# Nine first-layer V batches in the load stage, and a ring of five tiles for the V rows

## The chip, the cores and the metric

The kernel runs on one core of a Trainium2 chip. Its time is the device time of one launch in microseconds (us), all loads of weights included. The engines are TensorE (PE; its weight loads are listed as PEld), VectorE (DVE), ScalarE (ACT), GpSimd (POOL) and the queue engine SyncE (SP). Each runs its own list of instructions in order. SP, ACT and POOL issue the DMA transfers.

## The reference

Two layers follow each other, with the same weights in both: a recurrent attention block A and a gated feed-forward block B, on 2048 rows of 512 columns in bf16.

```
def _A_ref(x, mem0, Wq, Wk, Wv, Wo, seg_len):       # H=32 heads, Dh=128, M=8, seg_len=32
    mem = mem0
    for s in range(n_seg):                          # 64 segments, one after the other
        h = concatenate([mem, xs], axis=1)          # 8 memory rows + 32 rows of x
        q, k, v = h @ Wq, h @ Wk, h @ Wv            # per head
        p = softmax(where(mask, q @ k^T * scale, -1e9))
        o = (p @ v) @ Wo
        mem = o[:, :M, :]                           # feeds the next segment
        outs.append(o[:, M:, :])
def _B_ref(x, ...):  return (sigmoid(x @ w_gate) * (x @ w_up)) @ w_down      # F = 1792

x = x + _A_ref(_layernorm(x), ...);  x = x + _B_ref(_layernorm(x), ...)      # layer 0
x = x + _A_ref(_layernorm(x), ...);  x = x + _B_ref(_layernorm(x), ...)      # layer 1
```

## The kernel before

**Steps.** Step t works on segment t of layer 0 and on segment t-6 of layer 1 together, so that one matmul streams 80 columns (40 of each layer). There are 70 steps. In steps 0 to 5 there is only layer 0, in steps 64 to 69 only layer 1. A step computes q and k (line 681, "QK"), the scores (700), the softmax on DVE and ACT (710 to 739), the transposed probabilities (750), the product with V (763, "PV") and the product with Wo (780), in five groups of six heads and one of two. It ends with the 8 memory rows, which step t+1 needs (line 793 or 798): the steps form a chain. Four segments are a block of 128 rows; a block's feed-forward (lines 844 and 863) and its layer norms run between the steps as filler.

**V.** Of a segment's 40 rows, 16 (the 8 memory rows and the first 8 of x) get their V in the step itself (the "strips", line 653). The other 24 rows per segment (96 per block) are computed ahead, for 128 rows at a time: a V pass (`v_pass`) is 8 evictions, and each eviction is 4 matmuls of 128x512 (line 557), a cast of 512 columns to a tile `vst`, and one or two DMAs (line 565) to a DRAM buffer `scr`. A step's rows come back by the loads `vsb<-scr` (line 643) into the tile `vsb`, from which PV takes its weights; the strips come from the tile `sst` (line 662). The buffers scr0 and scr1 belong to layers 0 and 1.

Layer 0's V rows can be computed at any time, since they need only the input x. Four blocks (384 rows) make three passes, a `v_group`. Before the change, groups [0,1,2,3] and [4,5,7,8] are written while the weights load ("boot"), and group [10,11,13,14] is given out after step 19. Blocks 6, 9, 12 and 15 fill the free 32 rows of layer 1's passes. In the boot stage the passes also use the six halves of the tiles `wd` as eviction buffers (`bootp`), and ACT issues the DMAs to scr instead of SP.

**Layer 1's V** is made just in time: block b's rows come out of layer 0's feed-forward, are normed, and the pass with tile `xvl` runs around the start of step 4b+6, which is also the step that first reads them. So in these steps V goes PE, cast, DMA to scr, DMA to vsb, PV.

**What sets the order.** Every piece of work is a task with an engine, a duration and a latency written in the code. A planner (`Planner`) places the tasks in ten rounds of list scheduling and keeps the round with the shortest planned span; the program is written in that order. For a DMA task the code gives the time until the data are there: 3500 ns for a write to scr (4500 in the boot stage), 3000 ns for a load of vsb. An engine's list is fixed: what is placed behind a waiting instruction waits too.

**DMA semaphores.** The DMAs of SP and ACT share eight semaphores (DMAHW0 to DMAHW7 in the rows below), given out in turn in the order of the program. A DMA is issued only when the one eight places ahead of it has landed.

Of the kernel before, what the change touches and what calls it, by code (L numbers as in the profile page):

```python
# [10 lines left out]
F32 = mybir.dt.float32  # L11
# [39 lines left out]
class Task:  # L51
    __slots__ = ("eng", "dur", "lat", "fn", "deps", "succ", "tail", "boost", "ndep", "ready", "start", "idx", "on", "fresh", "acq", "rel", "durs", "tick")

# [27 lines left out]
class Planner:  # L81
# [119 lines left out]
    def forward(self):  # L201
        T = self.tasks
        for bf in self.bufs:
            bf.first, bf.left, bf.slot, bf.t_free = None, len(set(bf.users)), None, 0.0
            bf.pool.free = [(0.0, None, i) for i in range(len(bf.pool.tiles))]
            bf.pool.used = {}
        free = {"PE": 0.0, "ACT": 0.0, "DVE": 0.0, "POOL": 0.0, "SP": 0.0}
        ready = {e: [] for e in free}
# [21 lines left out]
        for tk in T:  # L230
            tk.ndep = len(tk.deps)
            tk.ready = 0.0
            tk.on = None
            if tk.ndep == 0:
                release(tk)
# [5 lines left out]
        while left:  # L241
# [6 lines left out]
            for e in free:  # L248
# [19 lines left out]
                tk.tick = seq[e]  # L268
                if e in ("DVE", "ACT"):
                    end = now + tk.dur + self.WAIT * (self.waits(tk, seen[e]) > 1)  # L270
                else:
                    end = now + tk.dur
                free[e] = end
                heapq.heappush(events, (end, 1, 0))
                for bf in tk.acq:
                    pool = bf.pool
                    q = min((q for q in pool.free if self.slot_at(q, tk) <= now), key=lambda q: q[0])
                    pool.free.remove(q)
                    bf.slot = q[2]
                    bf.t_prev = q[1]  # L280
                    pool.used[bf.kind] = pool.used.get(bf.kind, 0) + 1
                for bf in tk.rel:
                    bf.left -= 1
# [30 lines left out]
    def waits(self, tk, seen):  # L314

        T = self.tasks
        need = {}
        for d in [T[i] for i in tk.deps]:
# [15 lines left out]
class Kern:  # L334
# [48 lines left out]
    def setup_tiles(self):  # L383
# [52 lines left out]
    def setup_consts(self):  # L436
        nc, tc = self.nc, self.tc
        with tc.tile_pool(name="tmp0", bufs=1) as tp0:
            identf = tp0.tile([P, P], F32, name="identf")
            cmasks.make_identity(nc, identf[:])  # L440
            nc.vector.tensor_copy(out=self.ident[:], in_=identf[:])
        NEG = -1.0e9 / self.scale
# [17 lines left out]
        for t_ in self.pb:  # L460
            nc.vector.memset(t_[:], 0.0)
        nc.gpsimd.memset(self.vsb[:], 0.0)

    def load_weights(self):
# [6 lines left out]
        def ld(dst, src, ns, keys):  # L471
            pl.add("SP", ns, lambda: nc.sync.dma_start(out=dst, in_=src), w=keys, boost=self.boot())

        for h0 in range(0, self.H, 8):
            cs = slice(h0 * P, (h0 + 8) * P)
            ld(self.wv[:, :, cs], wv_v[:, :, cs], P * self.DC * 8 * P * 2 / 300.0, [("wv", h) for h in range(h0, h0 + 8)])
        for g, (h0, gsz, us) in enumerate(self.groups):
            cs = slice(h0 * P, (h0 + gsz) * P)
            nb = P * self.DC * gsz * P * 2
            for nm, sb, v in (("wq", self.wq, wq_v), ("wk", self.wk, wk_v)):  # L480
                ld(sb[:, :, cs], v[:, :, cs], nb / 230.0, [(nm, h) for h in range(h0, h0 + gsz)])
            ld(self.wo[:, h0:h0 + gsz, :], wo_v[:, h0:h0 + gsz, :], P * gsz * self.D * 2 / 230.0, [("wo", h) for h in range(h0, h0 + gsz)])

# [22 lines left out]

    def layernorm_T(self, xb, xkey):
        nc, pl, D, DC = self.nc, self.pl, self.D, self.DC
        i = self.nxt("lns", 3)
        ln = self.lns[i]  # L510
        lk = ("lns", i)
        xn = pl.buf(self.xnp)
        pl.add("DVE", dve_ns(D), lambda: nc.vector.bn_stats(out=ln[:, 0:6], in_=xb), r=[xkey], w=[lk])
        pl.add("DVE", 100, lambda: nc.vector.bn_aggr(out=ln[:, 6:8], in_=ln[:, 0:6]), r=[lk], w=[lk])
# [4 lines left out]
        pl.add("ACT", act_ns(D) + 294, lambda: nc.scalar.activation(out=xn[:, :], in_=xb, func=ACTF.Identity, bias=ln[:, 10:11], scale=ln[:, 9:10]),  # L519
               r=[xkey, lk], w=[xn])  # L520
        B = pl.buf(self.bank, "bg")
# [26 lines left out]
    def v_pass(self, tile, keys, pieces, boot=False):  # L548

        nc, pl, DC = self.nc, self.pl, self.DC  # L550
        for k in range(self.H // 4):
# [10 lines left out]
            for c0, j, b, r0, n in pieces:  # L562
                d = self.scr[j][b * BLK * XS:(b + 1) * BLK * XS, cs].rearrange("(i r) e -> i r e", i=BLK)[:, r0:r0 + n, :]
                pl.add("ACT" if boot else "SP", 430, lambda vs=vs, d=d, c0=c0, n=n, q=nc.scalar if boot else nc.sync: (
                    q.dma_start(out=d, in_=vs[c0:c0 + BLK * n, :]), None)[1], lat=3500.0 + 1000.0 * boot,
                       r=[vs] + (["boot"] if boot else []), w=[("vd", j, b, q, k) for q in range(r0 // 8, (r0 + n) // 8)])

    def v_group(self, blocks, psts, boot=False):
# [5 lines left out]
        for b, cut in zip(blocks, cuts):  # L574
            pst, B = psts[b] if b in psts else self.ln_x(b, boot)
            for q, c0, r0, n in cut:
# [8 lines left out]

    def ln_x(self, b, boot=False):
        nc, pl = self.nc, self.pl
        i = self.nxt("xp", 2)
        xb, key = self.xp[i], (("xo", 0) if i == 0 else "xp1")
        pl.add("SP", 430, lambda: nc.sync.dma_start(out=xb[:], in_=self.x_in[b * P:(b + 1) * P, :]), w=[key], boost=(2e7 if boot else 0.0))  # L590
        return self.layernorm_T(xb[:], key)

# [17 lines left out]
    def emit_step(self, t):  # L610
# [26 lines left out]
        for j in jobs:  # L637
            s = t - j * LAG
            b, i = s // BLK, s % BLK
            row = KOFF if j == 0 else JOFF  # L640
            for k in range(2):
                cs = slice(k * 2048, (k + 1) * 2048)
                pl.add("SP", 430, lambda j=j, s=s, row=row, cs=cs: nc.sync.dma_start(
                    out=self.vsb[row:row + XS, cs], in_=self.scr[j][s * XS:(s + 1) * XS, cs]),
                    r=[("vd", j, b, q, kk) for q in range(3) for kk in range(4 * k, 4 * k + 4)], w=[("vx", j, k)], lat=3000.0)
        vb = [pl.buf(self.bank), pl.buf(self.bank)]
# [9 lines left out]
        def add_strips():  # L656
# [4 lines left out]
            for i in range(4):  # L661
                pl.add("SP", 430, lambda i=i: nc.sync.dma_start(
                    out=self.vsb[32:64, i * 1024:(i + 1) * 1024], in_=sb[32 * i:32 * i + 32, :, :]),
                       r=[(sb, 0), (sb, 1)], w=[("vs", i)], lat=3000.0, use=[sb])

        WB = pl.buf(self.bank)
        for g, (h0, gsz, us) in enumerate(self.groups):
# [92 lines left out]
            def pvm(h0=h0, gsz=gsz, ptsb=ptsb, OB=OB):  # L760
                for hl in range(gsz):
                    h = h0 + hl
                    nc.tensor.matmul(OB[:, hl * ncol:(hl + 1) * ncol], lhsT=self.vsb[:, h * P:(h + 1) * P],  # L763
                                     rhs=ptsb[:, hl, 0:ncol], start=True, stop=True)

            kk = range(h0 // 4, (h0 + gsz - 1) // 4 + 1)
            pl.add("PE", gsz * mm_ns(ncol), pvm, r=[("ptsb", pi)] + [("vs", k) for k in sorted({k // 2 for k in kk})] + [("vx", j, k) for k in sorted({k // 4 for k in kk}) for j in jobs], w=[OB])
            oi = self.nxt("otsb", 2)
# [38 lines left out]
    def ffn(self, j, b):  # L807
# [24 lines left out]
        for jp in range(FC // 2):  # L832
            gi = self.nxt("wg", self.NG)
            wg, wu = self.wg[gi], self.wu[gi]
            fs = slice(jp * 2 * P, (jp + 1) * 2 * P)
            pl.add("POOL", 1000, lambda wg=wg, fs=fs: nc.gpsimd.dma_start(out=wg[:], in_=self.wgv[:, :, fs]), w=[("wg", gi)], lat=3000.0)  # L836
            pl.add("POOL", 1000, lambda wu=wu, fs=fs: nc.gpsimd.dma_start(out=wu[:], in_=self.wuv[:, :, fs]), w=[("wu", gi)], lat=3000.0)  # L837
            GB = pl.buf(self.bank, "bg")
# [16 lines left out]
        for ip in range(FC // 2):  # L855
            di = self.nxt("wd", self.ND)
            wd = self.wd[di]
            pl.add("POOL", 1000, lambda wd=wd, ip=ip: nc.gpsimd.dma_start(out=wd[:], in_=self.wdv[:, 2 * ip:2 * ip + 2, :]), w=[("wd", di)] + (["boot"] if self.cnt["wd"] <= self.ND else []), lat=3000.0)  # L858

# [26 lines left out]
    def trace(self):  # L886
        self.fill = {}
        self.load_mem0()
        p0 = self.pre1(0)
        p1 = self.pre1(1)  # L890
        self.load_weights()
# [89 lines left out]
```

## Time and profile before

| | |
|---|---|
| median of three runs | 2004.15 us (2001.04 to 2006.01) |
| the profiled execution | 2000.2 us, of which the span of the program's instructions is 1998.4 |
| mean granted TensorE clock | 0.977 |
| PE busy | 1832.3 us (92%) |
| DVE, ACT, POOL busy | 67%, 57%, 27% |
| DMA moved | 273.78 MB, 137 GB/s |
| the last matmul of step 0 | ends at 119.7 us |
| steps 1 to 69 | some 17 to 53 us each |

The page and the views are to be read as follows. A group's row gives busy time, mean duration and the idle time of its engine just before it with what ended it. Rows of a timeline give start and length; "ACTq" and "SPq" are the issuing of DMAs by those engines, in which the engine itself is idle. A windows row gives for a stretch of time the busy time of each engine, then the granted clock, the mean share of the DMA engines that was busy, and the bytes per time.

### The profile page before, as it was taken

What the parts mean: (1) busy time and instruction counts of PE and PEld (TensorE: products, weight loads), DVE (VectorE), ACT (ScalarE), POOL (GpSimd) and SP (SyncE); (2) the same over time, 40 slices, a digit from 0 to 9 for tenths busy, and PEclk for the clock granted to TensorE, in tenths of its full rate; (3) what the DMA queues carried; (4) which work ended last, traced back from release to release, by engine and by line L of the source; (5) the groups of instructions that cost most, each with busy time, mean ns of one, the idle gap of its engine ahead of it and who ended that gap; (6) DMA issues with size and microseconds to landing.
All of it is one profiled execution on the core that took longest, in us unless ns stands there. A gap on an engine that the chain in (4) does not pass through costs nothing.

```text
span 1998.4 us, 93783 instructions
## 1 busy us (share of the span) xinstructions
PE 1832.3 (92%) x40904; PEld 1581.0 (79%) x41116; DVE 1335.8 (67%) x4353; ACT 1139.4 (57%) x2628; POOL 545.5 (27%) x765
## 2 busy tenths in 40 slices
PE   5679899999999999899999999999999999999987
PEld 2368787888878787787988888888889887988775
DVE  5466577676766675665777766677667677766764
ACT  2145565565655665565666656566665666665553
POOL 2001103233322223222322223242314232333322
PEclk8889999999999999999999999999999999999998
DMA  7823315455544455545545446464536454455534
GB/s 241 271 61 84 103 48 148 137 142 156 138 123 124 128 148 167 144 112 145 145 123 142 132 110 178 112 185 118 149 90 171 130 142 139 121 162 133 158 101 117
DMA packets 124319, 273.78 MB, mean 137 GB/s; under 512 B 23034, under 2 KB 63746, under 8 KB 123906
## 3 DMA queue, kind: packets, MB, share of 16 engines
q0 software_dynamic: 53760, 176.20, 31.5%
q1 hardware_dynamic: 63234, 85.26, 15.2%
q8 instruction: 322, 5.28, 1.2%
q10 hardware_dynamic: 6912, 6.29, 0.9%
q14 instruction: 91, 0.75, 0.1%
HBM read 222.04 MB, written 27.26 MB: 125 GB/s over the span
## 4 chain that ended last, share of the span: by engine, by line
PE 66%; DMA 14%; DVE 8%; issue 5%; ACT 3%; POOL 2%; SPq 1%; ACTq 0%; DVEq 0%; POOLq 0%
PE bank L681 24%; PE bank L780 13%; PE bank L844 7%; PE bank L653 5%; DMA scr<-vst 4%; PE bank L557 4%; PE bank L763 3%; PE bank L700 3%; PE bank L750 3%; PE bank L863 2%; DMA vsb<-scr 2%; DMA scr<-wd 2%; DVE st L710 1%; DMA wd<-in_B_w_down_dram 1%; DMA vsb<-sst 1%
## 5 line engine op out<-in xcount | busy, mean ns | idle before, releaser
L681 PE MATMUL bank<-hT,wq_sb 128*128 128x80 bf16 (+1 forms) x8960 | 625.0, 198 | 9.2 <-issue 2.8
L681 PE MATMUL bank<-hT,wk_sb 128*128 128x80 bf16 (+1 forms) x8960 | 624.9, 198 | 3.6 <-issue 2.0
L921 ACT CAST qku<-bank 128x480 bf16<-128x480 f32 (+3 forms) x770 | 392.9, 512 | 265.3 <-PE bank L681 229.9
L681 PEld LDWEIGHTS <-wq_sb 128*128 128x128 bf16 x8960 | 458.8, 99 | 31.5 <-issue 13.7
L681 PEld LDWEIGHTS <-wk_sb 128*128 128x128 bf16 x8960 | 452.0, 99 | 3.1 <-DMA wk_sb<-in_A_Wk_dram 1.7
L710 DVE TENSOR_TENSOR st<-bank,maskb 64x240 f32<-64x240 f32 (+5 forms) x768 | 283.4, 371 | 199.3 <-PE bank L700 190.2
L780 PE MATMUL bank<-otsb,wo_sb 128*128 128x80 bf16 (+1 forms) x8960 | 375.4, 200 | 5.9 <-ACT otsb L921 3.0
L780 PEld LDWEIGHTS <-wo_sb 128*128 128x128 bf16 x8960 | 346.0, 101 | 18.3 <-issue 8.4
L836 POOL DMA_DIRECT2D wg<-in_B_w_gate_dram x224 | 170.4, 761 | 561.2 <-PE bank L844 487.1
L921 ACT CAST otsb<-bank 128x480 bf16<-128x480 f32 (+3 forms) x420 | 198.6, 487 | 133.4 <-PE bank L763 98.7
L858 POOL DMA_DIRECT2D wd<-in_B_w_down_dram x224 | 159.4, 713 | 272.0 <-PE bank L750 95.6
L720 ACT ACTIVATE st<-st 104x240 f32<-104x240 f32 (+5 forms) x420 | 160.5, 384 | 100.5 <-DVE st L717 81.6
L736 DVE TENSOR_TENSOR pb<-st,rz 104x480 bf16<-104x480 f32 x348 | 206.8, 597 | 11.4 <-PE bank L750 7.1
L516 POOL TENSOR_TENSOR lns<-lns,negh 128x1 f32<-128x1 f32 x78 | 44.8, 576 | 608.3 <-DVE lns L515 498.6
L700 PE MATMUL bank<-qku 128*128 128x80 bf16 (+1 forms) x2240 | 170.2, 199 | 26.0 <-ACT qku L921 23.6
L722 DVE TENSOR_REDUCE sm<-st 104x6 f32<-104x240 f32 (+5 forms) x420 | 153.8, 368 | 59.9 <-ACT st L720 57.5
L921 ACT CAST ptsb<-bank 128x480 bf16<-128x480 f32 (+2 forms) x288 | 145.0, 508 | 63.1 <-PE bank L750 52.6
L763 PE MATMUL bank<-ptsb,vsb 128*128 128x80 bf16 (+1 forms) x2240 | 141.9, 201 | 41.9 <-DMA vsb<-scr 25.6
L844 PE MATMUL bank<-xnT,wg 128*128 128x128 bf16 x1792 | 176.7, 222 | 3.0 <-ACT xnT L921 1.1
L844 PE MATMUL bank<-xnT,wu 128*128 128x128 bf16 x1792 | 176.2, 222 | 1.6 <-DMA wu<-in_B_w_up_dram 1.6
L700 PEld LDWEIGHTS <-qku 128*128 128x128 bf16 x2240 | 117.5, 99 | 69.8 <-issue 22.1
L837 POOL DMA_DIRECT2D wu<-in_B_w_up_dram x224 | 167.9, 750 | 2.4 <-PE bank L844 1.1
(80 smaller groups left out, 2502.4 us busy)
## 6 DMA issues: line engine op xcount, KB each, us to landing
wg<-in_B_w_gate_dram POOLq DMA_DIRECT2D x224, 256.0 KB, 4.6
wu<-in_B_w_up_dram POOLq DMA_DIRECT2D x224, 256.0 KB, 5.0
wd<-in_B_w_down_dram POOLq DMA_DIRECT2D x224, 256.0 KB, 4.9
vsb<-scr SPq DMA_DIRECT2D x256, 96.0 KB
vsb<-sst SPq DMA_DIRECT2D x280, 64.0 KB
scr<-vst SPq DMA_DIRECT2D x144, 96.0 KB
wv_sb<-in_A_Wv_dram SPq DMA_DIRECT2D x4, 1024.0 KB
wq_sb<-in_A_Wq_dram SPq DMA_DIRECT2D x5, 768.0 KB
```

The lines of the kernel that those rows point to most:

```text
L681: nc.tensor.matmul(o_ap, lhsT=W[:, c, h * P:(h + 1) * P], rhs=mv(c), start=(c == 0), stop=(c == DC - 1))
L700: nc.tensor.matmul(s_all(SB)[:, uh - h0 + i, :], lhsT=qku[:, i, 0, :], rhs=fview(qku[:, i, 1, q0:q0 + 1], qc), start=True, stop=True)
L710: pl.add("DVE", dve_ns(n, True), lambda gsz=gsz, hs=hs, st=st, SB=SB, pj_=pj_, npj_=npj_, idx=idx: nc.vector.tensor_tensor(out=st[pj_, hs] ...
L720: pl.add("ACT", act_ns(n), lambda hs=hs, st=st: nc.scalar.activation(out=st[pr, hs], in_=st[pr, hs], func=ACTF.Exp, scale=self.scale), r=s ...
L736: nc.vector.tensor_tensor(out=o, in0=st[pr, hs].unsqueeze(1).to_broadcast([npart, 2, gsz, L]), in1=rz[pr, :, 0:gsz].unsqueeze(3).to_broadc ...
L763: nc.tensor.matmul(OB[:, hl * ncol:(hl + 1) * ncol], lhsT=self.vsb[:, h * P:(h + 1) * P], rhs=ptsb[:, hl, 0:ncol], start=True, stop=True)
L780: nc.tensor.matmul(WB[:, c * ncol:(c + 1) * ncol], lhsT=self.wo[:, h, c * P:(c + 1) * P], rhs=otsb[:, hl, 0:ncol], start=(h == 0 and c == ...
L836: pl.add("POOL", 1000, lambda wg=wg, fs=fs: nc.gpsimd.dma_start(out=wg[:], in_=self.wgv[:, :, fs]), w=[("wg", gi)], lat=3000.0)
L837: pl.add("POOL", 1000, lambda wu=wu, fs=fs: nc.gpsimd.dma_start(out=wu[:], in_=self.wuv[:, :, fs]), w=[("wu", gi)], lat=3000.0)
L844: nc.tensor.matmul(gu[:, 2 * i + k, :], lhsT=W[:, c, i * P:(i + 1) * P], rhs=xnT[:, c, :], start=(c == 0), stop=(c == DC - 1))
L858: pl.add("POOL", 1000, lambda wd=wd, ip=ip: nc.gpsimd.dma_start(out=wd[:], in_=self.wdv[:, 2 * ip:2 * ip + 2, :]), w=[("wd", di)] + (["boo ...
L921: nc.scalar.copy(out=dst, in_=src)
```

## The change

Five things change together.

1. Group [10,11,13,14] is given out in the boot stage too, so that all nine passes stand there. Their x blocks are fetched ahead, between the loads of Wv, into tiles that are idle at that time (`xs2` to `xs5`, `xa`, `oxT1`, `hff`), where before two tiles took turns.
2. `vsb`, one tile of 4096 columns, becomes a ring of five tiles of 1024 columns (8 heads). Chunk k of step t lies in tile (4t+k) mod 5. The loads `vsb<-scr` are four of 48 KB per layer and step instead of two of 96 KB, and each PV group waits for its own chunks.
3. The first loads of the feed-forward's weights (`wg`, `wu`) wait for the last load of Wo.
4. The planner's numbers: a write to scr 2600 ns (4600 in boot), a load of vsb 6000, of sst 2600, Wq, Wk and Wo at 180 GB/s instead of 230, a POOL DMA 760 ns to issue and 4000 to land instead of 1000 and 3000.
5. The planner counts a wait for a buffer's earlier users (`prev`) among the waits of an instruction.

The core of the diff:

```diff
-        self.vsb = c.tile([P, HE], BF16, name="vsb")
+        self.vsb = [c.tile([P, 1024], BF16, name=f"vsb{i}") for i in range(5)]
...
+        xb = list(self.boot_x)
         for h0 in range(0, self.H, 8):
             cs = slice(h0 * P, (h0 + 8) * P)
             ld(self.wv[:, :, cs], wv_v[:, :, cs], P * self.DC * 8 * P * 2 / 300.0, [("wv", h) for h in range(h0, h0 + 8)])
+            for b in xb[:3]:
+                self.load_x(b, *self.boot_x[b])
+            xb = xb[3:]
...
-                ld(sb[:, :, cs], v[:, :, cs], nb / 230.0, [(nm, h) for h in range(h0, h0 + gsz)])
+                ld(sb[:, :, cs], v[:, :, cs], nb / 180.0, [(nm, h) for h in range(h0, h0 + gsz)])
...
-                    q.dma_start(out=d, in_=vs[c0:c0 + BLK * n, :]), None)[1], lat=3500.0 + 1000.0 * boot,
+                    q.dma_start(out=d, in_=vs[c0:c0 + BLK * n, :]), None)[1], lat=2600.0 + 2000.0 * boot,
...
-            for k in range(2):
-                cs = slice(k * 2048, (k + 1) * 2048)
-                pl.add("SP", 430, lambda j=j, s=s, row=row, cs=cs: nc.sync.dma_start(
-                    out=self.vsb[row:row + XS, cs], in_=self.scr[j][s * XS:(s + 1) * XS, cs]),
-                    r=[("vd", j, b, q, kk) for q in range(3) for kk in range(4 * k, 4 * k + 4)], w=[("vx", j, k)], lat=3000.0)
+            for k in range(4):
+                cs = slice(k * 1024, (k + 1) * 1024)
+                vu = (4 * t + k) % 5
+                pl.add("SP", 430, lambda j=j, s=s, row=row, cs=cs, vu=vu: nc.sync.dma_start(
+                    out=self.vsb[vu][row:row + XS, :], in_=self.scr[j][s * XS:(s + 1) * XS, cs]),
+                    r=[("vd", j, b, q, kk) for q in range(3) for kk in (2 * k, 2 * k + 1)], w=[("vx", j, vu)], lat=6000.0)
...
+            kk = [(4 * t + k) % 5 for k in range(h0 // 8, (h0 + gsz - 1) // 8 + 1)]
+            pl.add("PE", gsz * mm_ns(ncol), pvm, r=[("ptsb", pi)] + [("vs", k) for k in kk] + [("vx", j, k) for k in kk for j in jobs], w=[OB])
...
+            pl.add("POOL", 760, lambda wg=wg, fs=fs: nc.gpsimd.dma_start(out=wg[:], in_=self.wgv[:, :, fs]), r=[("wo", self.H - 1)], w=[("wg", gi)], lat=4000.0)
...
         self.v_group([4, 5, 7, 8], {}, True)
+        self.v_group([10, 11, 13, 14], {}, True)
...
-                if b == 4:
-                    self.v_group([10, 11, 13, 14], {})
```

What the planner makes of it is seen in three places of the programs. The first is ACT's list at the end of step 0: the last writes to scr (line 565 before, 572 after), the casts of q and k (`qku`, six heads are two casts of 6x40, the last two heads one cast of 4x40) and the exponential (`st`). Before:

```order
L565 DMA scr0_60<-wd0_133 96x512
L565 DMA scr0_60<-vst1_124 4x8x512
L565 DMA scr0_60<-vst1_124 96x512
L921 CAST qku2_80<-bank7_149 128x6x40
L921 CAST qku0_78<-bank4_146 128x6x40
L720 ACTIVATE st0_82<-st0_82 64x240
L921 CAST qku1_79<-bank5_147 128x4x40
L720 ACTIVATE st1_83<-st1_83 64x80
```

And after, at the same place:

```order
L940 CAST qku0_78<-bank5_151 128x6x40
L572 DMA scr0_60<-wd1_138 96x512
L572 DMA scr0_60<-wd2_139 4x8x512
L572 DMA scr0_60<-wd2_139 96x512
L572 DMA scr0_60<-wd0_137 4x8x512
L572 DMA scr0_60<-wd0_137 96x512
L572 DMA scr0_60<-vst0_127 4x8x512
L572 DMA scr0_60<-vst0_127 96x512
L735 ACTIVATE st0_86<-st0_86 64x240
L572 DMA scr0_60<-wd1_138 4x8x512
L572 DMA scr0_60<-wd1_138 96x512
```

The casts of the last group of six heads now stand ahead of the last eleven writes; behind the last write only the cast of the last two heads remains. Counted through the lists up to the last of these writes, ACT has 96 writes to scr before and 144 after. In the common order of all engines 75 of the 96 stand ahead of the last load of Wo, and 55 of the 144; so 21 stand behind it before, and 89 after, with 21 other ACT instructions among them (four before).

The second place is SP's list at step 26, where the group that is moved had its writes to scr0 (pieces of 4x16 rows, or of 96 and 4x8), next to those of layer 1's pass to scr1. Before:

```order
L565 DMA scr0_60<-vst1_124 4x16x512 [waits DMAHW6_49,DVE_49]
L565 DMA scr0_60<-vst1_124 4x16x512 [waits DMAHW7_49]
L565 DMA scr0_60<-vst2_125 4x8x512 [waits DMAHW0_49,Activation_49]
L565 DMA scr0_60<-vst2_125 96x512 [waits DMAHW1_49]
L565 DMA scr1_61<-vst0_123 96x512 [waits DMAHW2_49,DVE_49]
L565 DMA scr0_60<-vst0_123 4x8x512 [waits DMAHW3_49]
L662 DMA vsb_81<-sst0_126 32x1024 [waits DMAHW4_49,DVE_49,Activation_49]
```

And after, in the same step:

```order
L657 DMA vsb3_84<-scr0_60 24x1024 [waits DMAHW6_49,PE_49]
L572 DMA scr1_61<-vst1_128 96x512 [waits DMAHW7_49,Activation_49]
L572 DMA scr0_60<-vst1_128 4x8x512 [waits DMAHW0_49]
L572 DMA scr1_61<-vst2_129 96x512 [waits DMAHW1_49,Activation_49]
L657 DMA vsb4_85<-scr1_61 24x1024 [waits DMAHW7_49,DMAHW2_49,DMAHW1_49]
```

The group's writes are gone from there, and so are its 24 evictions and 96 matmuls on PE, which stood in steps 22 to 28; all nine passes now stand in step 0.

The third place is SP's list at step 30, one of the steps 4b+6 in which layer 1's V rows are made and read. Each eviction writes 96 rows to scr1 and 4x8 filler rows to scr0. Before:

```order
L565 DMA scr1_61<-vst0_123 96x512 [waits DMAHW5_49,Activation_49]
L643 DMA vsb_81<-scr1_61 24x2048 [waits DMAHW5_49,DMAHW6_49,DMAHW3_49,DMAHW1_49]
L565 DMA scr0_60<-vst0_123 4x8x512 [waits DMAHW7_49]
L565 DMA scr1_61<-vst1_124 96x512 [waits DMAHW0_49,Activation_49]
L565 DMA scr0_60<-vst1_124 4x8x512
L565 DMA scr1_61<-vst2_125 96x512 [waits DMAHW2_49,Activation_49]
L565 DMA scr0_60<-vst2_125 4x8x512
L565 DMA scr1_61<-vst0_123 96x512 [waits DMAHW4_49,DVE_49]
L565 DMA scr0_60<-vst0_123 4x8x512
L565 DMA scr1_61<-vst1_124 96x512 [waits DMAHW6_49,Activation_49]
L643 DMA vsb_81<-scr1_61 24x2048 [waits DMAHW6_49,DMAHW4_49,DMAHW7_49,DMAHW2_49,DMAHW0_49]
```

And after:

```order
L657 DMA vsb0_81<-scr1_61 24x1024 [waits DMAHW5_49,DMAHW4_49,DMAHW2_49]
L657 DMA vsb4_85<-scr1_61 24x1024 [waits DMAHW6_49]
L572 DMA scr0_60<-vst1_128 4x8x512 [waits DMAHW7_49]
L572 DMA scr1_61<-vst2_129 96x512 [waits DMAHW0_49,Activation_49]
L572 DMA scr0_60<-vst2_129 4x8x512 [waits DMAHW1_49]
L572 DMA scr1_61<-vst0_127 96x512 [waits Activation_49]
L657 DMA vsb1_82<-scr1_61 24x1024 [waits DMAHW3_49,DMAHW2_49,DMAHW0_49]
L572 DMA scr0_60<-vst0_127 4x8x512
L572 DMA scr1_61<-vst1_128 96x512 [waits DMAHW5_49,Activation_49]
L572 DMA scr0_60<-vst1_128 4x8x512 [waits DMAHW6_49]
L572 DMA scr1_61<-vst2_129 96x512 [waits DMAHW7_49,Activation_49]
L657 DMA vsb2_83<-scr1_61 24x1024 [waits DMAHW7_49,DMAHW5_49]
```

Before, the first half is loaded after the fourth eviction and the second half after the eighth. After, the four chunks are loaded after the second, fourth, sixth and eighth (the last load stands nine rows further on), and the four strips' loads for this step, which stood between the first and the second eviction, now stand between the sixth and the eighth. On PE the pass itself starts earlier: its first eviction stands at the end of step 29 and its second at the start of step 30 (before: four matmuls at the start of step 30, and the other seven evictions through the first half of the step, the last one just ahead of the first PV).

More of the change, by code (lines that the diff above doesn't have):

```diff
@@ L233, in forward @@
             tk.on = None
+            tk.prev = []
             if tk.ndep == 0:
@@ L279, in forward @@
                     bf.slot = q[2]
-                    bf.t_prev = q[1]
+                    tk.prev += pool.last.get(q[2], [])
+                    pool.last[q[2]] = sorted(set(bf.users))
                     pool.used[bf.kind] = pool.used.get(bf.kind, 0) + 1
+                end = now + tk.dur
+                if self.waits(tk, seen[e]) > 1 and e in ("DVE", "ACT"):
+                    end += self.WAIT
+                free[e] = end
+                heapq.heappush(events, (end, 1, 0))
                 for bf in tk.rel:
@@ L461, in setup_consts @@
             nc.vector.memset(t_[:], 0.0)
-        nc.gpsimd.memset(self.vsb[:], 0.0)
+        for t_ in self.vsb:
+            nc.gpsimd.memset(t_[:], 0.0)
     def load_weights(self):
```

65 lines of the change are left out of this document (34 added, 31 removed).

## Prediction

> **What bounds the kernel now.** I read the page's head first, then busy time by stretches cut at step ends, then who waited for whom, then the timelines of ACT, SP and PE at the places of the change.
>
> ```profile
> span 1998.4 us, 93783 instructions
> PE 1832.3 (92%) x40904; PEld 1581.0 (79%) x41116; DVE 1335.8 (67%) x4353; ACT 1139.4 (57%) x2628; POOL 545.5 (27%) x765
> ```
>
> ```profile
> 0.00:119.70 119.70, 69.94 (x735) 38.70 (x745) 58.80 (x154) 23.92 (x52) 18.33 (x33) 0.84 0.71 232
> ...
> 543.00:906.80 363.80, 339.11 (x7146) 290.09 (x7184) 240.63 (x784) 212.82 (x472) 102.17 (x143) 0.99 0.49 136
> 906.80:1235.60 328.80, 315.36 (x7036) 279.73 (x7072) 231.70 (x752) 200.84 (x454) 100.32 (x139) 0.99 0.51 140
> 1235.60:1563.40 327.80, 312.47 (x7027) 276.61 (x7070) 229.47 (x753) 201.04 (x447) 99.84 (x138) 1.00 0.50 140
> ```
>
> After its label and length a row gives the busy time of PE, PEld, DVE, ACT and POOL, the clock, the DMA share and GB/s. The first row is step 0: PE is idle for 49.8 of 119.7 us and the DMA engines are 71% busy. The others are twelve steps each (18 to 29, 30 to 41, 42 to 53). There PE is busy 93 to 96% of the time, so work taken from PE's list there shortens the kernel. Steps 18 to 29 hold the group that is moved.
>
> ```profile
> PE bank L763 <- DMA vsb<-scr: 25.6, 16, 4.1
> PE bank L700 <- ACT qku L921: 23.6, 17, 6.6
> ```
>
> Past step 0 the largest wait of PE is the first row: PV stands for V rows on their way back from DRAM, 16 times, 1.6 us each, at most 4.1. The second row is mostly step 0, where ACT's casts stand behind ACT's own writes to scr.
>
> **The change part by part.**
>
> *The group leaves steps 22 to 28.* Steps 18 to 29 take 363.8 us, the next twelve, with the same recurrent and feed-forward work, 328.8: 35.0 us more. That splits into 23.75 us of PE busy time (339.11 less 315.36) and 11.25 of idle time (24.7 less 13.4). The V line alone shows the busy part:
>
> ```profile
> 543.00:906.80 363.80, 46.48 (x177) 17.14 (x192) 0.99 0.49 136
> 906.80:1235.60 328.80, 21.91 (x84) 8.14 (x96) 0.99 0.51 140
> ```
>
> 192 weight loads against 96: the 96 matmuls of the group take 24.6 us. The 24 casts, four layer norms and four x loads go too. I take all 35.0. Bounds: 23.75, if the extra idle time belongs to the planner's choice there, and 35.0.
>
> *The group comes into step 0.* PE has 49.8 us free for 24.6 us of matmuls, so PE is not what counts; ACT's list is. ACT issues every write to scr in this stage, and its casts and exponentials stand in the same list:
>
> ```profile
> 97.16 0.36 ACT L921 CAST qku<-bank 128x240 bf16<-128x240 f32 x1 [6.33 <-DMA scr<-wd]
> 97.23 0.60 ACTq L565 DMA_DIRECT2D scr<-wd  x1
> 97.88 0.36 ACT L921 CAST qku<-bank 128x240 bf16<-128x240 f32 x1 [0.37 <-issue]
> 97.94 0.40 ACTq L565 DMA_DIRECT2D scr<-wd  x1
> 98.43 1.19 ACTq L565 DMA_DIRECT2D scr<-vst  x2
> 99.71 1.11 ACTq L565 DMA_DIRECT2D scr<-wd  x2
> 101.05 1.11 ACTq L565 DMA_DIRECT2D scr<-vst  x2
> 102.42 0.60 ACTq L565 DMA_DIRECT2D scr<-wd  x1
> 103.07 0.40 ACT L720 ACTIVATE st<-st 64x240 f32<-64x240 f32 x1 [4.83 <-DMA scr<-wd]
> 103.36 0.31 ACTq L565 DMA_DIRECT2D scr<-wd  x1
> 103.77 1.09 ACTq L565 DMA_DIRECT2D scr<-vst  x2
> ```
>
> Here no weight is in flight any more, and ACT issues almost without a pause: 12 writes and three operations (1.12 us) in 7.70 us, 0.55 us for each write. So the issuing itself is the pace (median 0.526 us):
>
> ```profile
> L565 ACTq DMA_DIRECT2D scr<-wd x60: 310/526/691, 23.7 to 103.4; - x60
> ...
> L565 ACTq DMA_DIRECT2D scr<-vst x36: 310/526/1190, 18.2 to 104.4; - x36
> ```
>
> When do the weights end? The loads of Wq, Wk and Wo go out between these two rows of SP, at 275 GB/s:
>
> ```profile
> 24.17 0.38 SPq L472 DMA_DIRECT2D wq_sb<-in_A_Wq_dram  x1
> ...
> 87.93 0.37 SPq L472 DMA_DIRECT2D wo_sb<-in_A_Wo_dram  x1
> ```
>
> ```profile
> 24.10:88.30 64.20, 45.58 (x377) 22.91 (x382) 32.34 (x77) 11.98 (x24) 2.16 (x4) 0.87 0.83 275
> 88.30:104.90 16.60, 7.18 (x74) 3.50 (x75) 5.99 (x13) 1.48 (x4) 0.00 (x0) 0.79 0.56 174
> ```
>
> In the new order 55 writes instead of 68 lie between them (13 x 64 KB is 0.85 MB, 3 us less), and ahead of them six loads of gate and up weights go (1.57 MB) and four x blocks come (0.52 MB), 4 us less. So the last Wo load goes out near 81 us. Then 89 writes follow in ACT's list instead of 21: 89 x 0.55 is 49 us, the 21 ACT operations among them take 9 us (seven casts of 0.36, four exponentials of 0.40, three norms of 0.81 and others), and 2 us I add for waits while weights still land: the last write near 141 us instead of 104.9. After it the old order needed 14.8 us to the end of step 0, since the last group of six heads came behind it; the new order has only the last two heads behind it, as from this row on:
>
> ```profile
> 111.93 0.29 ACT L921 CAST qku<-bank 128x160 bf16<-128x160 f32 x1 [2.34 <-PE bank L681]
> ```
>
> From there to 119.7 it was 7.8 us; the transposes that stand ahead of the first PV now add some 2. Step 0 would end at 151 instead of 119.7: plus 31. Bounds: ACT without any wait from its first write at 18.2 us needs 144 x 0.55 and some 18 us of operations (of the 23.92 that it is busy in step 0), so ends at 115 us, and 10 more, plus 6; at the pace of the whole old tail (16.6 us for 21 writes, 0.79 us each) 81 + 70 + 10, plus 41.
>
> The Trainium skill (DMA: Bandwidth & Descriptors, Rules for kernel authors) says that DMAs of SP, ACT and GpSimd run on the same 16 engines, so that spreading them saves only issue time. By that rule the bytes would set the price of step 0, which is the first rival below; the 0.83 DMA share while weights load agrees with it, the 0.56 after them does not.
>
> *x fetched ahead.* Ten x loads move ahead of the weights on SP; counted above. It removes waits such as PE's for `xn`, which lie in step 0 and are covered by ACT's list: 0.
>
> *The ring.* In step 30, PV of heads 16 and up waited for the second half of vsb, which SP could issue only when the eighth eviction had landed in scr (SP's, then PE's timeline, then the chain):
>
> ```profile
> 933.54 0.29 SPq L643 DMA_DIRECT2D vsb<-scr  x1
> ```
>
> ```profile
> 933.83 0.31 PE L763 MATMUL bank<-ptsb,vsb 128*128 128x80 bf16 x4
> 937.79 1.09 PE L763 MATMUL bank<-ptsb,vsb 128*128 128x80 bf16 x14 [3.65 <-DMA vsb<-scr]
> ```
>
> ```profile
> 929.94 3.46 DMA scr<-vst
> 933.54 4.12 DMA vsb<-scr
> ```
>
> Now heads 16 to 23 need only six evictions, the pass starts in step 29, and the planner allows 8.6 us for the two transfers, which take 7.6 here (it allowed 6.5). I take two thirds of the 25.6 us as gone, minus 17. Not all, since the write and the load still follow each other with 7.6 us. Bounds: minus 25.6 and plus 25.6 (rival three).
>
> The skill's same section says to join small transfers, and that below 64 KB one pays mostly overhead: the ring's 48 KB loads go against it. By the rule a load would still take about the 4.12 us of the 96 KB one, so I count nothing for the smaller size.
>
> *SP, POOL, numbers.* SP gets up to four more issues per step of 0.29 us (the row above), 1.2 us where twelve steps take 328: hidden, unless SP stands (rival three). Gate and up loads start after Wo; step 4 is the first to use them, and the rest of step 0 with steps 1 to 3 is the cover. The planner's other numbers only move filler: within plus or minus 4.
>
> Sum: -35 + 31 - 17 = -21 us. On the profiled execution's 2000.2 us that is 1979; its own time lies 4 us under the median of the runs, 2004.15, so the median should come to 1983.
>
> **The rivals.**
>
> *Step 0 is limited by bytes, not by ACT.* 48 more writes of 64 KB and four x blocks less six weight loads are 2.1 MB, 8 us at 275 GB/s: -35 + 8 - 17 gives 1960. For it: the share of 0.83 while weights load. Against it: 89 of the 144 writes stand behind the last load, where the share was 0.56.
>
> *The stalls stay.* Evictions and the round trip through DRAM remain, and a stall that moves from the second half to a chunk is still a stall: -35 + 31 + 0 gives 2000, within what can be measured. For it: the 7.6 us of the two transfers in the chain, which the ring does not shorten. Against it: the pass starts earlier on PE, and the last wait shown was for the eighth eviction.
>
> *SP becomes the wait: slower.* In steps 4b+6 SP has four loads instead of two that stand until a write has landed, and all later writes, and the strips, stand behind them; with three tiles `vst` the casts then stand, and DVE and ACT with them. If the stalls double, +25.6: -35 + 31 + 26 gives 2026. It decides from 4 us of added stalls on. For it: 3.46 us per write, where the planner now counts 2.6. Against it: SP is otherwise far from full.
>
> **How the numbers follow.** The sum above has 0.48, with 1972 to 1996 as its own range; bytes 0.18; stalls stay 0.18; SP stands 0.16. What differs by less than 0.3%, about 6 us, can't be told from no change. So faster takes the first two cases and a sixth of the third, less 0.01: 0.68; same most of the third and a little of the fourth: 0.15; slower the rest, 0.17. The range goes from 1958 to 2006: it takes in the bytes case and the case in which the stalls stay, and leaves out the fourth and the outer bounds.
>
> **What would show it.** Right: step 0 ending near 150 us with ACT issuing scr writes at 0.55 us each up to about 140; twelve steps 18 to 29 of about 328 us; PE's wait for `vsb<-scr` below 12 us; the V line with 288 `xvf` matmuls all in step 0. Wrong: step 0 ending below 132 us (bytes), or PE waits for vsb, or casts waiting for `scr<-vst`, above 30 us in all (SP).

## The result and the profile after

The changed kernel takes 1946.7 us (median; 1945.5 to 1950.0) where the kernel before took 2003.2 beside it: a ratio of 0.972, interval 0.970 to 0.974. The forecast was 1983 with a range from 1958 to 2006. Faster was right; the gain is 56 us and not 21.

The head of the page after the change:

```profile
span 1948.3 us, 94182 instructions
PE 1817.5 (93%) x40901; PEld 1568.3 (80%) x41116; DVE 1327.0 (68%) x4329; ACT 1152.9 (59%) x2652; POOL 549.5 (28%) x769
```

Busy time by stretches, cut as before: step 0, steps 18 to 29, 30 to 41, 42 to 53.

```profile
0.00:148.25 148.25, 95.55 (x845) 48.65 (x857) 79.37 (x194) 28.13 (x62) 21.64 (x41) 0.85 0.67 213
559.70:885.20 325.50, 314.10 (x7035) 278.94 (x7074) 225.49 (x746) 207.15 (x461) 100.85 (x139) 0.99 0.51 142
885.20:1204.80 319.60, 311.51 (x7035) 276.28 (x7070) 228.78 (x749) 204.77 (x456) 100.81 (x139) 1.00 0.51 143
1204.80:1525.40 320.60, 312.32 (x7035) 276.73 (x7074) 223.92 (x741) 206.59 (x462) 100.68 (x138) 1.00 0.52 144
```

Step 0 is longer by 28.5 us and steps 18 to 29 are shorter by 38.3; both were forecast (31 and 35). But the stretches that the group never touched are shorter too, 319.6 for 328.8 and 320.6 for 327.8. In the list of PE's waits there is no row for `vsb<-scr` any more (25.6 us before). Of the rows that are left, the first lies in step 0 for the most part, and the largest for vsb is that of the strips:

```profile
PE bank L715 <- ACT qku L940: 20.1, 11, 8.8
...
PE bank L778 <- DMA vsb<-sst: 8.3, 13, 1.3
```

Something else went with the waits. These are four stretches of 3.4 us around the wait of 3.65 us in step 30 of the kernel before (busy time of PE, then the granted clock):

```profile
930.60:934.05 3.45, 3.40 (x62) 1.00 0.82 221
934.05:937.46 3.41, 0.09 (x3) 1.00 0.94 269
937.46:940.87 3.41, 3.08 (x42) 0.50 0.92 234
940.87:944.28 3.41, 3.36 (x81) 1.00 0.37 101
```

PE stands in the second. In the third it works, but at half the clock: 42 matmuls where the next stretch has 81. So this wait cost its own 3.65 us and then some 1.7 us more, half of a stretch. Before, steps 1 to 61 hold ten such half-clock stretches; after, two (one of double length).

With this the time of any stretch splits into three parts: PE's idle times of over 0.2 us, the clock lost (half of each half-clock stretch), and the rest, which I call work. The table is worked out in this way from the profiled execution of each kernel, in us; only the median is over all of its runs, and a single execution lies up to 8 us from it (e5: 1951 and 1959):

| kernel | median | step 0 | steps 1 to 61 | = work | + idle | + clock | steps 62 on |
|---|---|---|---|---|---|---|---|
| before | 2003 | 119.7 | 1661.7 | 1570.8 | 73.9 | 17.1 | 217.0 |
| after | 1947 | 148.3 | 1589.6 | 1542.6 | 41.9 | 5.1 | 210.4 |
| e2: after, old numbers | 2029 | 126.6 | 1693.6 | 1543.1 | 111.2 | 39.3 | 210.9 |
| e4: after, group late | 1960 | 123.5 | 1626.0 | 1561.8 | 52.2 | 11.9 | 209.0 |
| e5: before, vsb load 6000 | 1959 | 121.4 | 1617.6 | 1574.2 | 38.3 | 5.1 | 210.3 |
| e6: before, ring | 2016 | 122.1 | 1676.6 | 1568.6 | 84.1 | 23.9 | 217.1 |
| e8: after, 230 GB/s, no prev | 1934 | 130.3 | 1585.9 | 1548.9 | 31.9 | 5.1 | 211.5 |

The work of steps 30 to 61 alone lies between 836 and 845 us in all 17 kernels profiled, while these steps take 846 to 907. So the kernels differ by idle time and clock there, not by what PE has to do. From before to after steps 1 to 61 lose 28 us of work (the moved group), 32 of idle time and 12 of clock.

### The profile page after: what moved, and what is told of

It reads as the page before. It is cut to its first block, busy times and chain, and to the rows that moved or that the text cites. A ratio compares the mean times of both kernels' runs of the same rounds, so it can differ in the third digit from the quotient of the medians.

```text
span 1948.3 us, 94182 instructions
## 1 busy us (share of the span) xinstructions
PE 1817.5 (93%) x40901; PEld 1568.3 (80%) x41116; DVE 1327.0 (68%) x4329; ACT 1152.9 (59%) x2652; POOL 549.5 (28%) x769
## 4 chain that ended last, share of the span: by engine, by line
PE 75%; DVE 9%; DMA 7%; ACT 4%; issue 3%; POOL 1%; ACTq 1%; SPq 0%; DVEq 0%; POOLq 0%
PE bank L696 27%; PE bank L795 14%; PE bank L859 9%; PE bank L564 6%; PE bank L667 5%; PE bank L715 3%; PE bank L765 3%; PE bank L878 3%; PE bank L778 3%; DMA vsb<-sst 2%; DVE st L725 2%; DMA scr<-vst 1%; DVE mx L730 1%; DVE pb L751 1%; DVE sm L737 1%
## 5 line engine op out<-in xcount | busy, mean ns | idle before, releaser
L795 PEld LDWEIGHTS <-wo_sb 128*128 128x128 bf16 x8960 | 341.5, 99 | 20.6 <-issue 10.6
L940 ACT CAST ptsb<-bank 128x480 bf16<-128x480 f32 (+3 forms) x316 | 157.0, 503 | 55.5 <-PE bank L765 42.9
L715 PE MATMUL bank<-qku 128*128 128x80 bf16 (+1 forms) x2240 | 170.1, 199 | 20.8 <-ACT qku L940 20.1
L765 PE MATMUL bank<-ident,pb 128*128 128x80 bf16 (+1 forms) x2240 | 144.1, 198 | 20.3 <-DVE pb L754 15.8
```

Source lines behind the costliest of these rows:

```text
L715: nc.tensor.matmul(s_all(SB)[:, uh - h0 + i, :], lhsT=qku[:, i, 0, :], rhs=fview(qku[:, i, 1, q0:q0 + 1], qc), start=True, stop=True)
L765: nc.tensor.matmul(o_ap, lhsT=pb[:, hl, :], rhs=idn, start=True, stop=True)
L795: nc.tensor.matmul(WB[:, c * ncol:(c + 1) * ncol], lhsT=self.wo[:, h, c * P:(c + 1) * P], rhs=otsb[:, hl, 0:ncol], start=(h == 0 and c == ...
L940: nc.scalar.copy(out=dst, in_=src)
```

## The experiments

All of them compute the whole reference. Each was timed beside the kernel before, which had medians of 1999.8 to 2003.2 us.

### Which part brought the gain: four parts undone one at a time

My theory was the ring with the price of the clock added; the main rival was the planner's number for a load of vsb.

e1, the changed kernel with the single tile and its two loads of 96 KB, the number for a load still at 6000:

```diff
-        self.vsb = [c.tile([P, 1024], BF16, name=f"vsb{i}") for i in range(5)]
+        self.vsb = c.tile([P, HE], BF16, name="vsb")
...
-            for k in range(4):
-                cs = slice(k * 1024, (k + 1) * 1024)
+            for k in range(2):
+                cs = slice(k * 2048, (k + 1) * 2048)
```

> The changed kernel with the old single tile vsb (two loads of 96 KB per layer and step, PV of heads 16 and up behind the second half), all else as after the change, the planner's 6000 ns for a vsb load too. My theory (the ring took the stalls away, and each stall cost more than its wait, because the granted clock was halved for 3.4 us after it): PE's wait for vsb<-scr returns to 20 us or more, with six or more half-clock stretches between steps 6 and 62, and the time goes from 1947 to 1980 (1970 to 1990). Rival (the planner's 6000 ns did it, by starting the V passes a step earlier): the wait stays under 8 us and the time between 1943 and 1955.

1958.0 us, ratio 0.978 (0.973 to 0.983). Without the ring most of the gain stays, and PE's list has no row for `vsb<-scr`. The theory fell; the rival was right on the wait, and the time is 3 us above its range.

e2, the changed kernel with all old numbers (those for sst and POOL, not shown, too):

```diff
-lat=2600.0 + 2000.0 * boot,
+lat=3500.0 + 1000.0 * boot,
...
-w=[("vx", j, vu)], lat=6000.0)
+w=[("vx", j, vu)], lat=3000.0)
...
-nb / 180.0
+nb / 230.0
```

> The changed kernel with all of the planner's old numbers (write to scr 3500 ns, 4500 in the load stage, vsb load 3000, sst 3000, weights at 230 GB/s, POOL DMA 1000 and 3000); ring, group and accounting stay. My theory (ring): 1943 to 1957, the wait for vsb<-scr under 6 us. Rival (numbers): the passes slide back into steps 4b+6, the wait for vsb<-scr is 15 us or more, and the time is 1970 to 1990.

2029.0 us, ratio 1.012 (1.006 to 1.018): slower than before. The rival's direction, and more than it said. The first row of PE's waits in e2:

```profile
PE bank L778 <- DMA vsb<-scr: 68.3, 32, 8.1
```

The other four parts together, without the numbers, more than double the waits. The half-clock stretches, 17 with some of several times 3.41 us, take another 39 us.

e3, without the new accounting:

```diff
-        for d in [T[i] for i in list(tk.deps) + tk.prev]:
+        for d in [T[i] for i in list(tk.deps)]:
```

> The changed kernel without the planner's new counting of a buffer's earlier users as waits (prev); all else stays. My theory: 1941 to 1955, since this only shifts some casts by fractions of a microsecond. Rival (the accounting made the regular plan of 106 us per block): 1960 or more, with PE idle times of 4 us or more back in several steps.

1939.4 us, ratio 0.968 (0.962 to 0.974), 2 us under my range. The accounting did not make the regular plan. That leaving it out seems to gain 7 us is taken up below.

e4, the group late (the fetches of its x blocks, not shown, go back with it):

```diff
-        self.v_group([10, 11, 13, 14], {}, True)
...
+                if b == 4:
+                    self.v_group([10, 11, 13, 14], {})
```

> The changed kernel with group [10,11,13,14] given out after step 19 again, as before the change; ring, numbers and accounting stay. Step 0 should end near 120 us instead of 148 (28 us earlier) and steps 18 to 29 take 350 to 364 us instead of 326. If the group costs there what it cost before the change (38 us): 1957 (1950 to 1962). Rival (with the ring the group costs its PE time alone, 24 to 27 us): 1943 to 1948, so that moving it brought nothing. Second rival (the group also unsettled the later steps): 1965 or more.

1960.4 us, ratio 0.979 (0.974 to 0.985); step 0 ends at 123.5, and steps 18 to 29 are as long as they ever were (their row of busy time in e4):

```profile
532.50:897.40 364.90, 339.48 (x7141) 290.81 (x7186) 234.73 (x771) 220.89 (x488) 102.35 (x143) 0.98 0.48 136
```

So the group costs 39 us there and 25 in step 0: moving it is worth about 14 of the 56 us, as far as one pair of plans can tell.

### The number and the ring, each alone on the kernel before

e5, one number:

```diff
-                    r=[("vd", j, b, q, kk) ...], w=[("vx", j, k)], lat=3000.0)
+                    r=[("vd", j, b, q, kk) ...], w=[("vx", j, k)], lat=6000.0)
```

> The kernel before with one number changed: the planner counts 6000 ns for a load of vsb instead of 3000. No ring, no moved group. My theory after the first four runs (this number alone removes the waits, because PV is then planned behind other work until the rows are there): PE's wait for vsb<-scr falls from 25.6 to below 5 us, seven half-clock stretches go, and the time falls by 30 to 38 us, to 1966 (1960 to 1975). Rival (the number only helps with the finer chunks of the ring): the wait stays at 15 us or more and the time between 1990 and 2005.

1959.0 us, ratio 0.979 (0.975 to 0.983), 1 us better than the range of my theory. A single number in the planner brings 42 us, three quarters of the gain. Only the order of the program differs, and which of ACT and DVE does a cast. PE's list has no row for `vsb<-scr`. How the order does it is seen in step 30. In the kernel before, the last matmuls of the V pass stand here, 19.6 us after the step's start, behind all of the step's q and k:

```profile
926.41 1.03 PE L557 MATMUL bank<-wv_sb,xvl 128*128 128x512 bf16 x4
```

From here to the PV that waits (937.79, shown in the prediction) stood the scores, PV and Wo products of the first heads and filler, 6.7 us in all, and they did not last. In e5 the same matmuls and the PV that reads the second half of vsb:

```profile
902.82 1.04 PE L557 MATMUL bank<-wv_sb,xvl 128*128 128x512 bf16 x4
...
911.67 0.59 PE L763 MATMUL bank<-ptsb,vsb 128*128 128x80 bf16 x12
```

They begin 16 us after the step's start. Sixteen rows of four q or k matmuls, then work of the first heads and filler stand between them and PV, which waits for nothing. In the planner's code a task's rank is at first the longest way behind it, latencies included. The larger number so raises the rank of all that stands ahead of the load: V matmuls, casts and writes. Here the pass ends ahead of the last q and k instead of behind them. Over the eight steps 30, 34 ... 58 the last V matmul ends 19.5 us after the step's start before, and 14.7 in e5; the first PV starts at 20.0 and 20.8.

e6, the ring alone (four loads of 48 KB, waits by chunk, lat=3000; the two lines of e1 the other way round):

> The kernel before with the ring of five tiles alone: four loads of 48 KB per layer and step, PV waits by chunk; the planner's old numbers, the old place of the group. If the finer dependences by themselves do harm under the old number (as the 68 us of waits in the run with the old numbers suggest): wait for vsb<-scr 50 us or more, 2040 (2025 to 2060). Rival (those waits came from the group or from the planner's accounting, and the ring alone helps as I first forecast): wait 8 to 15 us, 1980 to 1992.

2016.5 us, ratio 1.008 (1.006 to 1.010): slower, but less than I had written, and the wait for vsb is hardly larger than before:

```profile
PE bank L702 <- ACT qku L923: 38.4, 22, 7.3
PE bank L765 <- DMA vsb<-scr: 27.4, 19, 3.5
```

The first row was 23.6 us before (past step 0 it is 20.0 here and was 6.8): other waits grow. The casts to `vst` wait 42.8 us in all for writes to scr to land, where it was 19.2 before, as the third rival of the prediction had it. Whether the longer waits of PE come from that these runs do not tell.

e9, a smaller step of the number:

```diff
-   w=[("vx", j, k)], lat=3000.0
+   w=[("vx", j, k)], lat=4500.0
```

> The kernel before with the planner counting 4500 ns for a load of vsb (3000 before, 6000 after). Theory (the number works by covering the true way of write and load, 7.6 us in the trace of before: 3500 + 3000 is too short, 3500 + 4500 = 8.0 is just enough): PE's wait for vsb<-scr below 6 us, at most four half-clock stretches in steps 1 to 61, 1960 (1953 to 1968), the same as with 6000. Rival (every microsecond planned buys a share, since the pass is only ranked higher): half of the gain, wait 8 to 15 us, 1975 to 1985.

1953.7 us, ratio 0.977 (0.973 to 0.980), wait 1.5 us. Half the step gives the whole gain. The theory held in time and wait, though five half-clock stretches remained, where at most four were forecast.

Its reason did not hold. The 7.6 us are those of step 30, the longest of the eight steps 30, 34 ... 58. From the issue of the eighth eviction's write to the start of the PV of heads 16 and up the kernel before took 4.1 to 7.9 us, and under 6 us in all steps but this one: less than the 3500 + 3000 ns of its plan. That PV waited in six of the eight all the same. In e9 this way is no shorter (means 5.3 and 5.2 us), and PV waits in none. What moved is the start of the way. These are the casts of the eighth eviction in step 42, before and in e9:

```profile
1257.83 0.64 DVE L923 CAST vst<-bank 128x512 bf16<-128x512 f32 x1
```

```profile
1222.78 0.58 ACT L921 CAST vst<-bank 128x512 bf16<-128x512 f32 x1
```

The last V matmul had ended at 1255.58 and at 1222.70, so the cast came 2.25 us later before, and 0.08 in e9. Over the eight steps the write went out 2.6 us after that matmul before and 1.0 in e9, on the mean, while the matmul itself ends only 0.6 us earlier (18.9 after 19.5). So in these steps the number worked less through PE's order than through that of the casts on ACT and DVE. No number between 3000 and 4500 was run, so where the gain sets in stays open.

e10, ring and number on the kernel before:

> The kernel before with the ring of five tiles and the 6000 ns together. This completes the square: before 2001, ring alone 2016, number alone 1959. Theory (the finer chunks help once no PV stands for them): 1948 (1941 to 1954), as in the changed kernel, where the ring was worth 11 us. First rival (the ring does nothing more where no wait is left): 1955 to 1963. Second rival (the ring costs its 15 us here as well): 1970 to 1980.

1952.8 us, ratio 0.975 (0.972 to 0.978), within the range of my theory, but only 6 us under e5. The square: 2001 before, 2016 ring, 1959 number, 1953 both.

### Is a difference of 5 to 10 us an effect or another plan?

The planner searches, so any edit gives another plan. e12 and e13 change 6000 to 5500 and 6500 in the changed kernel; e14 and e15 repeat e3 and e1 with 6500.

> The changed kernel with 5500 ns instead of 6000 for a load of vsb: a step that should change nothing of substance, since 2600 + 5500 = 8.1 us still covers the 7.6 us of the true way. It shows how much another plan of equal quality moves the time. If differences of 5 to 10 us between kernels are real effects: 1944 to 1950. Rival (the plan found by ten rounds of search scatters): below 1941 or above 1953.

> The same with 6500 ns. Effects real: 1944 to 1950. Rival (scatter of the plans): below 1941 or above 1953.

> The changed kernel without the new accounting (prev), with 6500 ns. If leaving prev out is worth 7 us by itself: 1937 to 1942 and some 7 us under the run with prev and 6500. Rival (the 7 us were the scatter of two plans): the two with 6500 lie within 4 us of each other, or the other way round.

> The changed kernel with the old single tile vsb and 6500 ns. If the ring is worth 11 us in the changed kernel: 1955 to 1961, some 8 to 14 us over the ring with 6500. Rival (scatter): within 5 us of it.

| | 5500 | 6000 | 6500 |
|---|---|---|---|
| the changed kernel | 1940.3 | 1946.7 | 1947.6 |
| without prev | | 1939.4 (e3) | 1947.3 (e14) |
| with one tile | | 1958.0 (e1) | 1952.0 (e15) |

Plans of equal substance lie 7 us apart, so the rival of e12 came true. The 7 us of e3 do not repeat (0.3 us in e14): scatter. The ring's 11 us become 4, and 6 on the kernel before: three times the same sign, but hardly larger than the scatter, so its size stays open. The 14 us of the group (e4) are twice the scatter, the 42 us of the number six times.

### What sets the end of step 0

e7, the changed kernel with the old numbers but for the 6000:

> The changed kernel with all of the planner's old numbers except the 6000 ns for a vsb load. Theory (this number carries the gain of the steps, and the old 230 GB/s for the weights gives the shorter step 0 of 127 us seen with the old numbers): wait for vsb<-scr below 5 us, steps 1 to 69 as after the change plus some of the third group's V work that now runs after step 0, 1935 (1925 to 1946). First rival (what step 0 saves is only work put off, and comes back in steps 1 to 4): 1944 to 1952. Second rival (the 2600 ns for a write, 760 and 4000 ns for POOL carry a part too): 1955 or more.

1937.8 us, ratio 0.969 (0.965 to 0.973); step 0 ends at 133.7 us, not at 127. The theory held in the time and on its main point: the other numbers carry no gain.

e8, 230 GB/s for the weights, without prev:

```diff
-nb / 180.0
+nb / 230.0
...
-        for d in [T[i] for i in list(tk.deps) + tk.prev]:
+        for d in [T[i] for i in list(tk.deps)]:
```

> The changed kernel with two things undone: the weights are planned at 230 GB/s again, and the new accounting (prev) is left out. If a step 0 of about 127 us and the smoother steps without prev add up: 1922 (1915 to 1932), better than both kernels. Rival (step 0 does not shorten by the weights' number alone): 1936 to 1944, as without prev alone.

1934.2 us, ratio 0.967 (0.963 to 0.972), between my range and the rival's. It differs from e3 by the weights' number alone, and step 0 is shorter by 17.5 us. For e3 follow the row of busy time of step 0 and the larger part of ACT's writes to scr (shortest, median and longest duration of one, then the first and the last start):

```profile
0.00:147.80 147.80, 97.01 (x845) 49.14 (x857) 79.93 (x193) 27.30 (x64) 21.58 (x41) 0.85 0.66 213
```

```profile
L572 ACTq DMA_DIRECT2D scr<-wd x96: 310/526/1024, 21.9 to 138.6; - x96
```

The same two for e8 (the first with PE alone):

```profile
0.00:130.30 130.30, 90.22 (x833) 0.88 0.70 227
```

```profile
L572 ACTq DMA_DIRECT2D scr<-wd x96: 310/526/997, 22.0 to 148.7; - x96
```

In e3 all 144 writes lie ahead of step 0's end; in e8 ACT needs even longer, but 14 writes and 18 of the V matmuls stand behind that end, in step 1. So ACT's list was long, as forecast, and still did not have to set the end of step 0: what the order puts ahead of that end did. Of the 17.5 us some 12 are left in the span, and 5 between the medians.

e11, e8 with SP issuing the third group's writes:

```diff
-                pl.add("ACT" if boot else "SP", 430, ...
+                pl.add("ACT" if boot == 1 else "SP", 430, ...
...
-        self.v_group([10, 11, 13, 14], {}, True)
+        self.v_group([10, 11, 13, 14], {}, 2)
```

> The best kernel so far (the changed kernel, weights planned at 230 GB/s, without prev), in which SP instead of ACT issues the 48 writes to scr of the third group in the load stage. If ACT's list of writes, casts and exponentials sets the end of step 0: step 0 ends at 118 us (110 to 124) instead of 130, and the time is 1922 (1914 to 1928). Rival (the bytes or the casts and PE set it): step 0 ends at 127 to 132 and the time is 1929 to 1937. Second rival (SP now stands for casts, and the loads of vsb behind it come late): step 0 ends at 135 or later, 1938 or more.

1941.5 us, ratio 0.970 (0.967 to 0.973); step 0 is no shorter than in e8 (its row of e11):

```profile
0.00:129.90 129.90, 84.60 (x793) 44.04 (x806) 67.03 (x174) 28.76 (x63) 18.80 (x37) 0.86 0.66 214
```

48 fewer writes on ACT gain nothing. The planner puts 28 more V matmuls behind step 0 (46 of their weight loads, where e8 has 18), and steps 1 to 17 take 12.8 us longer. The rival for step 0 and the second rival's time came true.

The best version is e8. It lies 0.6% under the changed kernel; the intervals overlap, and the scatter of plans is of that size. What is firm in it is the shorter step 0, which e2 and e7, planned at 230 GB/s too, also show.

## Why the prediction was wrong, step by step

*The group leaves.* Forecast -35 for steps 18 to 29, measured -38.3, and e4 gives 39 for the same undone. PE busy fell by 25.0 there (339.11 to 314.10; forecast 23.75). Right.

*The group comes into step 0.* Forecast +31, measured +28.5. The parts were near as well. The last Wo load went out earlier than the forecast 81 us:

```profile
71.33 0.37 SPq L474 DMA_DIRECT2D wo_sb<-in_A_Wo_dram  x1
```

Behind it stand 90 writes (89 forecast) and 20 operations of 9.0 us (21 and 9), the last write at 138.8 us (141). So the pace was 0.75 us per write with all that lies between, and 0.65 without the operations, slower than the 0.55 that I had said, and the earlier start made up for it. But the reason was half wrong: e8 has the same 144 writes on ACT and ends step 0 at 130 us. Some 17 us of the 28.5 are the 180 GB/s, which I had booked at nothing. The bytes rival is not shown by that either. Step 0 ended 7 to 14 us later than before in e2, e7 and e8, near its 8, but with 11 to 17 writes put off to step 1, and no run changed the bytes.

*The ring, -17: the step that failed.* I took the ring for the cause and the numbers for filler, "within plus or minus 4". It is the other way round: the number for a vsb load alone brings 42 us (e5), the ring alone costs 15 (e6, one plan, twice the scatter), and with the number it may bring 4 to 11. I had written the number down (8.6 us in the new plan, 6.5 in the old, 7.6 in the trace), but followed the wait to the dependence that the ring makes finer, and not to the order that the planner makes from the number. And the 7.6 us were one step's, the longest of eight: in most steps the casts came late, and the transfers were shorter than planned (see e9).

*The price of a wait.* The waits for vsb were booked at their own 25.6 us. PE's idle time in steps 1 to 61 fell by 32 us, near the 28 that the forecast's terms hold (11.25 and 17). Not in any term: 12 us of lost clock, 6.6 us in the steps from 62 on, and some 4 us more work. These with 4 more of idle time and 2.5 less in step 0 are the 29 us between the forecast sum of -21 and the -50 of the two profiled spans. The medians lie 56 apart: the profiled execution of before (2000.2) is 3 us under its median, that of after (1950.0) 3 us over.

*x fetched ahead, the feed-forward loads behind Wo.* Never tested alone; nothing in the profile after shows a price for them.

*The rivals.* "SP becomes the wait" named a slower time of 2026 for a change whose stalls double: that is the size of what the change does without the numbers (e2, 68.3 us of waits, 2029). There SP stands 150.8 us for writes ahead of its loads of vsb, 60.8 before, which fits the rival; no run separates SP's list from the rest of the order. The ring alone (e6) leaves the wait for vsb at 27.4 us, which is nearer to "the stalls stay". The signs that I had named as right (PE's wait below 12 us, steps 18 to 29 at 328, step 0 near 150, writes until 140) came true but for the pace of the writes. They would have for either cause: they could not tell ring from number.

## What to carry to other kernels

Where a fixed order is made from planned latencies, compare the planned way of each chain that goes through DRAM with the way in the trace, in every step and from the matmul on, casts included, and try that one number alone before any change of tiles. Such a number also ranks the work ahead of the transfer: here a larger one brought the casts and writes forward and the waits went, although most transfers had been no longer than planned. Count a wait of PE of more than some 2 us at its length plus the clock that it loses, and let two plans that differ in nothing of substance show how much of a small gain is only another plan.

## What the runs showed of the hardware

The granted clock follows PE's idle time by a grid of 3.41 us. I cut steps 1 to 61 of all 17 profiled executions into stretches on that grid, laid through the changes of the clock, and added up PE's idle times of over 0.15 us in each stretch at full clock. Of some 7600 stretches with less than 0.75 us idle, none was followed by half a clock; of some 250 with 0.75 to 2.0 us, 35; of 49 with more than 2.0 us, all 49. The Trainium skill (TensorE: Matmul & The Clock Gate, Part 1) puts the drop after at least one idle window of about 3.4 us. Here less was enough: 2.0 us idle within a window, in several pieces too. By these counts, more than 2.0 us of waits within one stretch cost some 1.7 us on top (an estimate, half of the next stretch), a wait that falls on two stretches may not, and a stretch with less than 0.75 us of waits costs only these.
